# Two heads' softmax sums in one operation, and GpSimd's share of the weights given to ScalarE and VectorE

## The chip, the cores and the metric

The kernel runs on one core of one Trainium2 chip. Its time is device microseconds of one execution; the time of a kernel is the median of several. The core's engines work side by side, each through its own queue in order: TensorE (PE), VectorE (DVE), ScalarE (ACT), GpSimd (POOL) and SyncE (SP), which starts most of the DMAs. Some DMAs are started from ACT's queue.

## The reference

Attention over 4 batches of 8 heads, 576 positions of 64 values, with a learned relative bias; its output goes through a layer of three matrices with a maximum, and then a gated layer:

```python
scores = scale * np.matmul(q, k.transpose(0, 1, 3, 2))
...
scores = scores + bias.transpose(2, 0, 1)[None, :, :, :]
scores = scores - np.max(scores, axis=-1, keepdims=True)
attn = np.exp(scores)
attn = attn / (np.sum(attn, axis=-1, keepdims=True) + 1e-09)
return np.matmul(attn, v)
...
h = np.maximum(np.maximum(x @ w1, x @ w2), x @ w3) @ w_out
out = (sigmoid(h @ w_gate) * (h @ w_val)) @ moe2_w_out
```

All is float32; for the fast matrix products most operands are written as a sum of two 16-bit parts, a high and a low one.

## The kernel before, in words

The bias of all heads is made first and written to memory (to about 98 us). Then the attention runs in 160 steps. A *unit* is a tile of 128 (the last of a head 64) rows of one head; the units of two heads, an even and an odd one, alternate, so ten units make a *decade*: both heads of pair P, tiles 0 to 4, units 10P to 10P+9. Units u and u+1 with u even have the same rows of two heads. The 40 units of the first batch (`by_pe`, heads 0 to 7) go another way than the 120 after them.

The order on all queues is written out by hand: the loop `for u in range(NU + 7)` (L928) issues step u, and each helper takes the unit that is due in that step. In step u there are, in this order: `emit_E(u)` (DVE, L637: minimum of bias and scores, out of the accumulator memory), `emit_X(u)` (ACT, L643: the exponential, which also sums the row into `l`), the load of a later bias tile (ACT's queue), `emit_S(u+1)` (PE: scores, L617 and L618), `emit_r1(u-1)` (DVE, L648: the sum is scaled), `emit_hi2`, `emit_lo` and `emit_T` of units due, `emit_hi(u-1)` (DVE, L657: the reciprocal, and then the high part of the weights), evacuations of matrix products that are ready (`flush`), the product with v (`emit_V`), `prep(u)`, and then `feed.step`, which issues as much of the first layer of the batch before (`moe1`) as fills the step on PE. The fill is set by a table (`FEED`, 2.6 to 2.7 us a step) and doesn't look at what happens on the chip.

For the units after the first batch the weights go in one of two ways. Mostly ACT writes the high part out of exponential and reciprocal in step u+1 (L662), and DVE the low part in step u+2 (`emit_lo`, L677: product minus high part), and SP then starts a transposing DMA (`emit_T`, L702) from the weight buffer `ph` (five of them, `NPH`) to `pt`, from which PE takes its product with v. Where `by_pool(u)` is true (three of ten units in the second batch, two of ten in the third and fourth, 28 in all) GpSimd scales the exponential in place (L659), ACT casts it into the high part (L668), GpSimd subtracts (L674), and the transposing DMA is issued in step u+5. In the first batch GpSimd scales (L659 also) and PE transposes (`emit_TP`, L690).

`prep(u)` spreads the preparation of later heads over the steps. With s counted so that pair P's step s is u = 10P - 16 + s: SP loads q at s = 0 and k at s = 1 (`load_qk`, L359 and L360), into one buffer; ACT takes squares of them at s = 2 and 3 (`qk_squares`, L371); later DVE and POOL split them (L407, L402), SP transposes them (`r_trans`, L411) at the next decade's s = 0 and 1, and DVE swaps the halves of the transposed keys for each head (`k_swap`, L421 and L422) at s = 14 (even head) and 15 (odd head). The scores of the new pair's first two units need these: they are issued in the steps after. Because 10P - 16 is even, q is loaded in an even step and k in an odd one. For the pairs 2 to 5 the loads are issued six steps earlier; for pairs 6 to 15, ten decades, as said here.

What sets the lags: `e` tiles 4, `ph` tiles 5, two tiles of scores, and one tile each for raw q and k.

Of the kernel before, what the change touches and what calls it, by code (L numbers as in the profile page):

```python
# [10 lines left out]
F32 = mybir.dt.float32  # L11
# [3 lines left out]
AF = mybir.ActivationFunctionType  # L15
ALU = mybir.AluOpType
# [16 lines left out]
ESC = 16384.0  # L33
# [31 lines left out]
def tile_kernel(ctx, tc, q, k, v, w1, b1, w2, mw1, mw2, mw3, mwo, gw, vw, ow, xtab, masks, out):  # L65
    nc = tc.nc
# [38 lines left out]
    def tiny(n=1):  # L105
        for _ in range(min(n, len(tq))):
            tq.pop(0)()

    def end_tiny():
        tiny(len(tq))  # L110
# [26 lines left out]
    def take_sums():  # L137
        for then, g in summed:
            then(g)
        del summed[:]  # L140
# [20 lines left out]
    with tc.manual_schedule():  # L161
# [3 lines left out]
        PPB = H // 2  # L165
# [27 lines left out]
        def rpool(name, bufs):  # L193
            return at.enter_context(tc.tile_pool(name=name, bufs=bufs, side="right"))

        p1, p2, p3, p4 = rpool("p1", 1), rpool("p2", 2), rpool("p3", 3), rpool("p4", 4)
# [142 lines left out]
        def by_pe(n):  # L339
            return n < H  # L340
# [166 lines left out]
        units = []  # L507
# [3 lines left out]
        bias_t, e_t, ph_t, l_t, r_t, pt_t = {}, {}, {}, {}, {}, {}  # L511
# [93 lines left out]


        s_t, v_rest = {}, []

        def emit_S(u):

            n, it = units[u]
            m = rows[it]
            kq, k2 = kq_t[n], k2_t[n]
            ps = ps_s.tile([128, 1024], F32, tag="s", name="s")
            qs = kq[:, it, 0, :m]
            for j, kk in enumerate((kq[:, :, 1], k2)):
                nc.tensor.matmul(ps[:m, 0:512], lhsT=qs, rhs=kk[:, 0:4], start=(j == 0), stop=(j == 1))  # L617
                nc.tensor.matmul(ps[:m, 512:576], lhsT=qs, rhs=kk[:, 4, 0:64], start=(j == 0), stop=(j == 1))  # L618
            put_sums(ps[:, 600:616])
            s_t[u] = ps  # L620

        ep_t, x_t, n_ep = {}, {}, [0]

        def new_ep(u):
            ep_t[u] = ep_buf[n_ep[0] % len(ep_buf)]
            n_ep[0] += 1
            return ep_t[u]

        def emit_E(u):

            n, it = units[u]
            m = rows[it]
            ps = s_t.pop(u)
            e = new_ep(u)[:, 0:S] if by_pe(n) else p4.tile([128, S], F32, tag="e", name="e", bufs=NE)
            mx = p4.tile([128, 1], F32, tag="mx", name="mx")
            l = p4.tile([128, 1], F32, tag="l", name="l")
            nc.vector.tensor_tensor_reduce(e[:m], ps[:m, :S], bias_t.pop(u)[:m], -1.0, 3.0e38, ALU.add, ALU.min, mx[:m])  # L637
            e_t[u], l_t[u], x_t[u] = e, l, mx
            take_sums()

        def emit_X(u):
            m = rows[units[u][1]]
            nc.scalar.activation(e_t[u][:m], e_t[u][:m], AF.Exp, scale=-1.0, bias=x_t.pop(u)[:m], accum_out=l_t[u][:m])  # L643

        def emit_r1(u):
            m = rows[units[u][1]]
            r_t[u] = p4.tile([128, 1], F32, tag="r", name="r")
            nc.vector.tensor_scalar(r_t[u][:m], l_t.pop(u)[:m], 1e-9, 1.0 / ESC, op0=ALU.add, op1=ALU.mult)  # L648

        def by_pool(u):  # L650

            return u % 10 in ((2, 5, 8) if u < 20 * PPB else (2, 5)) and not by_pe(units[u][0])

        def emit_hi(u):
            m = rows[units[u][1]]
            r = r_t[u]
            nc.vector.reciprocal(r[:m], r[:m])  # L657
            if by_pool(u) or by_pe(units[u][0]):
                nc.gpsimd.tensor_scalar(e_t[u][:m], e_t[u][:m], r[:m], 1.0, op0=ALU.mult, op1=ALU.mult)  # L659
                return  # L660
            ph_t[u] = p3.tile([128, 2, S], F16, tag="ph", name="ph", bufs=NPH)
            nc.scalar.activation(ph_t[u][:m, 0], e_t[u][:m], AF.Copy, scale=r[:m])  # L662
# [7 lines left out]
        def emit_lo(u):  # L670
            m = rows[units[u][1]]
            ph = ph_t[u]
            if by_pool(u):
                nc.gpsimd.tensor_tensor(ph[:m, 1], e_t.pop(u)[:m], ph[:m, 0], op=ALU.subtract)  # L674
                r_t.pop(u)
            else:
                nc.vector.scalar_tensor_tensor(ph[:m, 1], e_t.pop(u)[:m], r_t.pop(u)[:m], ph[:m, 0], op0=ALU.mult, op1=ALU.subtract)  # L677
# [17 lines left out]
        def emit_T(u):  # L695
            n, it = units[u]
            m = rows[it]
            g, i0 = (0, 0) if it < 2 else (1, 2)
            if (n, g) not in pt_t:
                pt_t[n, g] = p1.tile([128, 9, (256, 320)[g]], F16, tag=f"pt{g}{n % 2}", name="pt")  # L700
            c0 = 128 * (it - i0)
            nc.sync.dma_start_transpose(out=pt_t[n, g][:, :, c0:c0 + m], in_=ph_t.pop(u)[:m].rearrange("p a s -> p (a s)"))  # L702
# [222 lines left out]
        def at_step(u, off):  # L925
            return [u - off] if 0 <= u - off < NU else []

        for u in range(NU + 7):  # L928
            t = FEED[u // (10 * PPB)]
            flush(both=False)  # L930
            if u == 10 * PPB + FIRST_MOE:
                flush()
                while late3:
                    late3.pop(0)[1]()
                psT.close()
                pools.update(mm=psA.enter_context(tc.tile_pool(name="ps_mm", bufs=4, space=PSUM)), n=4)
            if u == 0:
                emit_S(0)
            while late3 and late3[0][0] <= u:
                late3.pop(0)[1]()  # L940
            if u < NU:
                emit_E(u)
            for x in at_step(u, 0):
                emit_X(x)
            if u < NU:
                load_bias(u + NBI)
                t -= 0.49
            if u + 1 < NU:
                emit_S(u + 1)
            if v_rest:  # L950
                v_rest.pop(0)(u)
            tiny()
            for x in at_step(u, 1):
                emit_r1(x)
            for x in at_step(u, 5):
                if by_pool(x):
                    emit_T(x)
            for x in at_step(u, 2):
                emit_hi2(x)
                if not (by_pe(units[x][0]) or by_pool(x)):  # L960
                    emit_lo(x)
                    emit_T(x)
            tiny()
            for x in at_step(u, 1):
                emit_hi(x)
            for x in at_step(u, 3):
                if by_pool(x):
                    emit_lo(x)
                elif by_pe(units[x][0]):
                    emit_TP(x)  # L970
            flush()
            if slow:
                slow.pop(0)()
            for ua, g, late_, pe2 in ((3, 0, LA, False), (9, 1, LB, False), (3, 0, LA0, True), (9, 1, LB0, True)):
                w = u - ua - late_
                if w >= 0 and w % 10 == 0 and w // 10 < NP:
                    P = w // 10
                    if pe2 != (by_pe(2 * P) and by_pe(2 * P + 1)):
                        continue
                    if g == 0 and P % PPB == 0 and P // PPB >= 2:  # L980
                        while len(feed.q) > 1:
                            feed.one()
                        flush()
                        while slow:
                            slow.pop(0)()
                    emit_V(P, g, u)
                    if g == 1 and P % PPB == PPB - 1 and P < NP - 1:
                        xfer = P // PPB, max(u + (1 if P < PPB else 2), 10 * PPB + FIRST_MOE)
                    t -= (1.9, 2.3)[g]
            if xfer is not None and u >= xfer[1]:  # L990
                feed.q.append(moe1(xfer[0], x2[xfer[0]]))
                xfer = None
            prep(u)
            if u == 34:
                for _ in side_work:
                    force_ring()
                    end_tiny()
                common_scales()
            if u >= 6 and u % 2 == 0:
                next(side_work, None)  # L1000
            if u == 10 * PPB:
                w64_o = [t.bitcast(I32).rearrange("p (f t) -> p f t", t=2) for t in
                         (slots[3][:, 1536:3072], fx2[:, 0:1536], fx2[:, 1536:3072], fx2[:, 0:1536])]
                out_work = first_weights((3,), w64_o, {3: quarters(fx2[:, 3072:6144])}, 2)
                next(out_work)
            if u >= 10 * PPB + OUT_AT:
                next(out_work, None)
            feed.step(t)
# [265 lines left out]
```

## Time and profile before

| | us |
|---|---|
| three runs | 1093.58, 1082.88, 1083.96 |
| median | 1083.96 |
| profiled execution, its time | 1085.36 |
| its span, first to last instruction | 1083.5 |
| PE busy in the span | 995.3 |
| DVE busy | 689.5 |
| ACT busy | 549.1 |
| POOL busy | 189.1 |

An engine's busy time is a sum over stages; what counts in a stage is which wait ends last there. A row of a timeline gives start, duration, engine, line and operation, output and inputs, and in brackets the idle time before it with what ended it. PE, DVE, ACT, POOL stand for the engines, SPq for the queue of SP, whose rows are the starts of DMAs.

### The profile page before, as it was taken

How to read it: one execution, taken by the hardware profiler on the slowest of the kernel's cores; microseconds unless marked ns; L12 is line 12 of the kernel's file. 1: busy time of each engine (PE TensorE's matmuls, PEld its weight loads, DVE VectorE, ACT ScalarE, POOL GpSimd, SP SyncE). 2: the span in 40 equal slices, each digit the busy share in tenths (PEclk: the TensorE clock that was granted, in tenths of full speed). 3: DMA queues.
4: the chain of work that ended last, by engine and by line, in shares of the span. 5: the costliest groups of instructions: out<-in, count | busy, mean ns of one | idle time of the engine just before them, and what ended most of it. 6: DMA issues, size and time to landing. Idle time of an engine off the chain costs nothing.

```text
span 1083.5 us, 20167 instructions
## 1 busy us (share of the span) xinstructions
PE 995.3 (92%) x7620; PEld 659.7 (61%) x7620; DVE 689.5 (64%) x1764; ACT 549.1 (51%) x1089; POOL 189.1 (17%) x199
## 2 busy tenths in 40 slices
PE   6977889878898899889999999998999999999998
PEld 2223445556665567656777777776764666766743
DVE  7997768889986889878866867778521221322210
ACT  6997778666775767776654435534410111211100
POOL 1003544343432244223321100000000000000000
PEclk9998989989998999999999999999999999999999
DMA  7898878999999999989964332323001000000001
GB/s 226 298 262 236 192 194 224 248 230 183 222 249 198 185 222 242 243 176 213 212 135 128 108 96 79 111 85 97 1 10 38 12 10 11 10 11 10 11 20 39
DMA packets 242958, 148.53 MB, mean 137 GB/s; under 512 B 183085, under 2 KB 214061, under 8 KB 242861
## 3 DMA queue, kind: packets, MB, share of 16 engines
q1 hardware_dynamic: 221604, 104.77, 45.2%
q10 hardware_dynamic: 21256, 42.48, 14.6%
q8 instruction: 60, 0.98, 0.4%
q14 instruction: 38, 0.30, 0.1%
HBM read 89.53 MB, written 15.34 MB: 97 GB/s over the span
## 4 chain that ended last, share of the span: by engine, by line
PE 53%; DVE 21%; DMA 10%; ACT 7%; issue 5%; ACTq 1%; POOL 1%; SPq 1%; DVEq 0%; POOLq 0%
PE po L1212 13%; PE mm L797 12%; PE pg L797 8%; PE pvl L797 8%; DMA pt<-ph 5%; PE s L797 3%; PE s L617 3%; PE t L690 2%; PE mm L756 2%; PE mm L752 2%; DVE xT L543 2%; DMA bias<-bias_d 2%; DVE e L637 2%; ACT ph L662 1%; DVE gT L1187 1%
## 5 line engine op out<-in xcount | busy, mean ns | idle before, releaser
L797 PEld LDWEIGHTS <-slot 128*128 128x128 f16 x2304 | 221.4, 99 | 88.2 <-issue 25.3
L797 PE MATMUL mm<-xT,slot 128*128 128x288 f16 x1512 | 212.1, 294 | 14.4 <-ACT hm L818 10.4
L1212 PE MATMUL po<-OW,gT 128*128 128x512 f16 x648 | 141.3, 379 | 0.0
L797 PEld LDWEIGHTS <-GW 128*128 128x128 f16 x1152 | 112.8, 98 | 41.7 <-issue 8.9
L797 PEld LDWEIGHTS <-VW 128*128 128x128 f16 x1152 | 112.2, 98 | 28.3
L643 ACT ACTIVATE e<-e,mx 128x576 f32<-128x576 f32 (+1 forms) x120 | 92.5, 771 | 46.2 <-DVE mx L637 42.5
L797 PE MATMUL pg<-x,GW 128*128 128x288 f16 x864 | 113.4, 289 | 0.5 <-DVE x_e L154 0.5
L797 PE MATMUL pvl<-x,VW 128*128 128x288 f16 x864 | 111.7, 286 | 0.0
L1177 ACT ACTIVATE sg<-pg,ug 128x576 f32<-128x576 f32 x48 | 35.5, 739 | 145.0 <-PE pg L797 131.4
L1212 PEld LDWEIGHTS <-gT 128*128 128x128 f16 x648 | 63.4, 98 | 74.8
L1184 DVE SCALAR_TENSOR_TENSOR sg<-pvl,sg 128x576 f32<-128x576 f32 x48 | 36.2, 754 | 108.4 <-PE pvl L797 107.6
L677 DVE SCALAR_TENSOR_TENSOR ph<-e,r,ph 128x576 f16<-128x576 f32 (+1 forms) x92 | 83.1, 903 | 22.5 <-ACT ph L662 22.3
L637 DVE CUSTOM_DVE_ANT_0 e<-s,bias 128x576 f32<-128x576 f32 (+1 forms) x120 | 89.5, 746 | 7.9 <-DMA bias<-bias_d 5.1
L1186 ACT CAST gT<-sg 128x576 f16<-128x576 f32 x48 | 32.2, 672 | 107.1 <-DVE sg L1184 107.1
L662 ACT ACTIVATE ph<-e,r 128x576 f16<-128x576 f32 (+1 forms) x92 | 71.0, 772 | 22.0 <-DMA pt<-ph 11.2
L552 PE MATMUL bo<-xT,w2blk 128*32 128x512 f32 x192 | 60.3, 622 | 16.9 <-DVE xT L543 14.3
L617 PE MATMUL s<-k,kq 128*128 128x512 f16 (+1 forms) x160 | 63.1, 394 | 13.2 <-DVE k L422 13.2
L1217 DVE TENSOR_TENSOR ob<-po,uo 128x512 f32<-128x512 f32 x16 | 11.1, 692 | 96.8 <-PE po L1212 96.8
L617 PE MATMUL s<-kq 128*128 128x512 f16 (+1 forms) x160 | 63.9, 399 | 8.4 <-DVE mx L637 5.9
L797 PE MATMUL mm<-hT,slot 128*128 128x288 f16 x504 | 66.1, 286 | 0.0
L1187 DVE TENSOR_TENSOR gT<-sg,gT 128x576 f16<-128x576 f32 x48 | 36.4, 759 | 34.9 <-ACT gT L1186 34.9
L617 PEld LDWEIGHTS <-kq 128*128 128x128 f16 (+1 forms) x320 | 32.7, 102 | 39.5 <-issue 17.4
(203 smaller groups left out, 1652.0 us busy)
## 6 DMA issues: line engine op xcount, KB each, us to landing
bias<-bias_d ACTq DMA_DIRECT2D x128, 288.0 KB, 4.1
bias_d<-x SPq DMA_DIRECT2D x36, 288.0 KB, 4.3
x<-in_moe_w_dram SPq DMA_DIRECT2D x12, 768.0 KB, 6.5
w<-in_moe_w_gate_dram SPq DMA_DIRECT2D x12, 512.0 KB, 3.8
w<-in_moe_w_val_dram SPq DMA_DIRECT2D x12, 512.0 KB, 3.6
w<-in_moe_w_out_dram SPq DMA_DIRECT2D x12, 512.0 KB, 3.4
bias<-bias_d ACTq DMA_DIRECT2D x32, 144.0 KB, 4.7
out_dram<-ob SPq DMA_DIRECT2D x36, 128.0 KB, 2.3
```

The costliest lines, as they stand in the source:

```text
L552: nc.tensor.matmul(bo[32 * g:32 * g + 32, 0:512], lhsT=lhsT, rhs=hs[4 * ti + g][:, :, 0:128], start=True, stop=True, tile_position=(0, 32 ...
L617: nc.tensor.matmul(ps[:m, 0:512], lhsT=qs, rhs=kk[:, 0:4], start=(j == 0), stop=(j == 1))
L637: nc.vector.tensor_tensor_reduce(e[:m], ps[:m, :S], bias_t.pop(u)[:m], -1.0, 3.0e38, ALU.add, ALU.min, mx[:m])
L643: nc.scalar.activation(e_t[u][:m], e_t[u][:m], AF.Exp, scale=-1.0, bias=x_t.pop(u)[:m], accum_out=l_t[u][:m])
L662: nc.scalar.activation(ph_t[u][:m, 0], e_t[u][:m], AF.Copy, scale=r[:m])
L677: nc.vector.scalar_tensor_tensor(ph[:m, 1], e_t.pop(u)[:m], r_t.pop(u)[:m], ph[:m, 0], op0=ALU.mult, op1=ALU.subtract)
L797: nc.tensor.matmul(ps[hf][:, :HS], lhsT=W(wp, kk), rhs=X(xp, kk)[:, hf * HS:(hf + 1) * HS], start=(first and i == 0), stop=(last and i == 2))
L1177: nc.scalar.activation(hm3(sg), pg[:, :, :HS], AF.Sigmoid, scale=ugm)
L1184: nc.vector.scalar_tensor_tensor(hm3(sg), pvl[:, :, :HS], DOWN2, hm3(sg), op0=ALU.mult, op1=ALU.mult)
L1186: nc.scalar.copy(gT[:, 0, m, c0:c0 + S], sg)
L1187: nc.vector.tensor_tensor(gT[:, 1, m, c0:c0 + S], sg, gT[:, 0, m, c0:c0 + S], op=ALU.subtract)
L1212: nc.tensor.matmul(po[:, 0, :], lhsT=gT[:, gi, kk, 128 * ct:128 * ct + 128], rhs=OW[:, wi, kk], start=(i == 0), stop=(i == 3 * K2 - 1))
```

## The change

The sum column `l` and the reciprocal `r` become tiles of two columns, one for each head of a pair of units. The scaling of sums and the reciprocal are done once for both, in the even step after the odd unit. `emit_hi` is issued for both units there, the odd one first; in the odd step that follows, `emit_lo` and `emit_T` are issued for both, the even one first. In the first batch the even unit's GpSimd scaling so moves one step later and behind the odd one's; `emit_TP` stays where it is. `by_pool` is false for every unit, so that from the second batch on ACT writes all high parts and DVE all low parts.

```diff
@@ emit_E @@
-            l = p4.tile([128, 1], F32, tag="l", name="l")
+            if u % 2 == 0:
+                l = p4.tile([128, 2], F32, tag="l", name="l")
+                l_t[u], l_t[u + 1] = l[:, 0:1], l[:, 1:2]
+                l2_t[u] = l
@@ emit_r1 @@
-            r_t[u] = p4.tile([128, 1], F32, tag="r", name="r")
-            nc.vector.tensor_scalar(r_t[u][:m], l_t.pop(u)[:m], 1e-9, 1.0 / ESC, op0=ALU.add, op1=ALU.mult)
+            if u % 2 == 0:
+                return
+            r = p4.tile([128, 2], F32, tag="r", name="r")
+            nc.vector.tensor_scalar(r[:m], l2_t.pop(u - 1)[:m], 1e-9, 1.0 / ESC, op0=ALU.add, op1=ALU.mult)
+            r_t[u - 1], r_t[u] = r[:, 0:1], r[:, 1:2]
+            r2_t[u] = r
@@ by_pool @@
-            return u % 10 in ((2, 5, 8) if u < 20 * PPB else (2, 5)) and not by_pe(units[u][0])
+            return False
@@ emit_hi @@
-            nc.vector.reciprocal(r[:m], r[:m])
+            if u in r2_t:
+                r2 = r2_t.pop(u)
+                nc.vector.reciprocal(r2[:m], r2[:m])
@@ step u @@
             for x in at_step(u, 2):
                 emit_hi2(x)
-                if not (by_pe(units[x][0]) or by_pool(x)):
-                    emit_lo(x)
-                    emit_T(x)
+            if u % 2:
+                for x in at_step(u, 3) + at_step(u, 2):
+                    if not (by_pe(units[x][0]) or by_pool(x)):
+                        emit_lo(x)
+                        emit_T(x)
             tiny()
             for x in at_step(u, 1):
-                emit_hi(x)
+                if x % 2:
+                    emit_hi(x)
+                    emit_hi(x - 1)
```

## Rows read from the trace of the kernel before

**Rows 1.** Busy time by stage, batches two to four (columns in the first line).

```profile
core 0: us, PE busy (x) PEld busy (x) DVE busy (x) ACT busy (x) POOL busy (x), PEclk, DMA share, GB/s
...
182.10:311.70 129.60, 110.85 (x892) 75.03 (x893) 114.11 (x311) 87.73 (x190) 50.63 (x46) 0.93 1.12 222
311.70:438.00 126.30, 114.10 (x978) 80.35 (x976) 104.93 (x302) 88.22 (x189) 41.18 (x39) 0.96 1.13 216
438.00:557.00 119.00, 110.12 (x965) 78.30 (x963) 100.90 (x290) 82.68 (x174) 36.55 (x36) 0.99 1.06 205
```

**Rows 2.** Waits in total: us, times, longest us.

```profile
PE s L617 <- DVE k L422: 13.2, 10, 2.8
...
ACT ph L662 <- DMA pt<-ph: 11.2, 5, 5.2
...
ACT junk_w L371 <- DMA rqk<-in_k_dram: 7.9, 6, 2.3
```

**Rows 3.** Groups of instructions: count, busy us, mean ns, idle before.

```profile
L677 DVE SCALAR_TENSOR_TENSOR ph<-e,r,ph 128x576 f16<-128x576 f32 (+1 forms) x92 | 83.1, 903 | 22.5 <-ACT ph L662 22.3
L662 ACT ACTIVATE ph<-e,r 128x576 f16<-128x576 f32 (+1 forms) x92 | 71.0, 772 | 22.0 <-DMA pt<-ph 11.2 <-ACT e L643 3.9 <-DVE R L407 1.9
...
L756 PE MATMUL mm<-pt,vh 128*64 128x256 f16 (+1 forms) x672 | 48.0, 294 | 7.1 <-DMA pt<-ph 4.3 <-ACT xT L855 1.5 <-DVE r L657 1.1
...
L674 POOL TENSOR_TENSOR ph<-e,ph 128x576 f16<-128x576 f32 (+1 forms) x28 | 37.1, 1326 | 35.4 <-ACT ph L668 30.5 <-DMA bias<-bias_d 4.5
...
L657 DVE RECIPROCAL r<-r 128x1 f32<-128x1 f32 (+1 forms) x160 | 24.9, 156 | 1.8
```

**Rows 4.** Timelines of DVE and of POOL, around 306 us.

```profile
306.25 1.26 DVE L677 SCALAR_TENSOR_TENSOR ph<-e,r,ph 128x576 f16<-128x576 f32 x1 [1.08 <-ACT ph L662]
...
305.62 1.28 POOL L674 TENSOR_TENSOR ph<-e,ph 128x576 f16<-128x576 f32 x1
```

**Rows 5.** Timeline of SP's queue, steps 102 to 105.

```profile
386.54 5.65 SPq L702 DMA_TRANSPOSE pt<-ph  x3
392.28 0.54 SPq L359 DMA_DIRECT2D rqk<-in_q_dram  x1
...
393.59 1.93 SPq L411 DMA_TRANSPOSE kq<-R  x1
395.62 3.14 SPq L702 DMA_TRANSPOSE pt<-ph  x1
398.81 0.58 SPq L359 DMA_DIRECT2D rqk<-in_k_dram  x1
```

**Rows 6.** Timeline of ACT, steps 107 and 108.

```profile
404.57 0.74 ACT L371 ACTIVATE junk_w<-rqk 128x640 bf16<-128x640 f32 x1 [1.06 <-DMA rqk<-in_k_dram]
...
405.30 0.76 ACT L643 ACTIVATE e<-e,mx 64x576 f32<-64x576 f32 x1
...
406.06 0.76 ACT L662 ACTIVATE ph<-e,r 128x576 f16<-128x576 f32 x1
```

**Rows 7.** Timeline of DVE, steps 103 and 109.

```profile
387.76 0.74 DVE L637 CUSTOM_DVE_ANT_0 e<-s,bias 128x576 f32<-128x576 f32 x1
...
407.07 0.80 DVE L677 SCALAR_TENSOR_TENSOR ph<-e,r,ph 128x576 f16<-128x576 f32 x1
...
408.47 0.48 DVE L422 COPY k<-kq 64x640 f16<-64x640 f16 x1
```

**Rows 8.** Timeline of PE, scores of unit 111.

```profile
409.23 0.38 PE L617 MATMUL s<-k,kq 128*128 128x512 f16 x1
```

**Rows 9.** A long wait of PE, and the stage of 6 us behind it.

```profile
343.29 3.18 PE L797 MATMUL mm<-xT,slot 128*128 128x288 f16 x12 [4.27 <-ACT hm L818]
...
342.00:348.00 6.00, 4.71 (x21) 2.67 (x21) 3.08 (x15) 3.19 (x6) 0.80 (x1) 0.54 1.14 226
```

**Rows 10.** Timelines of PE and POOL in the first batch, units 0, 1, 26, 27.

```profile
102.90 0.76 PE L690 MATMUL t<-hT,x 128*128 128x128 f32 x5 [1.10 <-POOL x L659]
...
104.16 2.74 POOL L659 TENSOR_SCALAR x<-x,r 128x576 f32<-128x576 f32 x3
...
159.21 0.74 POOL L659 TENSOR_SCALAR x<-x,r 128x576 f32<-128x576 f32 x1 [1.13 <-DVE r L657]
...
162.04 0.74 PE L690 MATMUL t<-hT,x 128*128 128x128 f32 x5 [0.35 <-ACT xT L692]
```

More of the change, by code (lines that the diff above doesn't have):

```diff
@@ L607, in tile_kernel @@
         s_t, v_rest = {}, []
+        l2_t, r2_t = {}, {}
         def emit_S(u):
@@ L635, in emit_E @@
             mx = p4.tile([128, 1], F32, tag="mx", name="mx")
-            l = p4.tile([128, 1], F32, tag="l", name="l")
+            if u % 2 == 0:
+                l = p4.tile([128, 2], F32, tag="l", name="l")
+                l_t[u], l_t[u + 1] = l[:, 0:1], l[:, 1:2]
+                l2_t[u] = l
             nc.vector.tensor_tensor_reduce(e[:m], ps[:m, :S], bias_t.pop(u)[:m], -1.0, 3.0e38, ALU.add, ALU.min, mx[:m])
-            e_t[u], l_t[u], x_t[u] = e, l, mx
+            e_t[u], x_t[u] = e, mx
             take_sums()
@@ L642, in emit_X @@
             m = rows[units[u][1]]
-            nc.scalar.activation(e_t[u][:m], e_t[u][:m], AF.Exp, scale=-1.0, bias=x_t.pop(u)[:m], accum_out=l_t[u][:m])
+            nc.scalar.activation(e_t[u][:m], e_t[u][:m], AF.Exp, scale=-1.0, bias=x_t.pop(u)[:m], accum_out=l_t.pop(u)[:m])
         def emit_r1(u):
             m = rows[units[u][1]]
-            r_t[u] = p4.tile([128, 1], F32, tag="r", name="r")
-            nc.vector.tensor_scalar(r_t[u][:m], l_t.pop(u)[:m], 1e-9, 1.0 / ESC, op0=ALU.add, op1=ALU.mult)
+            if u % 2 == 0:
[4 more added lines that the diff above has]
+            r2_t[u] = r
         def by_pool(u):
-            return u % 10 in ((2, 5, 8) if u < 20 * PPB else (2, 5)) and not by_pe(units[u][0])
+            return False
         def emit_hi(u):
```

## Prediction, made blind

> **What bounds the kernel now.** I read the page's slices and its busy table first, then the busy time by stage, then the waits in total, then the groups of instructions, and last the timelines of all queues over one stretch of ten steps. The busy time by stage [rows 1] shows the three batches that the change touches (heads 8 to 31, 40 steps each, a step being one tile of one head): they last 129.6, 126.3 and 119.0 us, 3.1 us a step. TensorE is busy for 111, 114 and 110 us of them and VectorE for 114, 105 and 101 us, so both are near the bound and ScalarE (88, 88, 83 us) is not. After 557 us TensorE works almost alone and nothing is changed there; time comes or goes only where TensorE is made to wait in these batches. The waits in total [rows 2] say for what it waits: 13.2 us in ten waits of the scores for the second VectorE copy of the swapped keys (L422). ScalarE waits 7.9 us in six for loaded keys (the squares, L371), and 11.2 us in five for a weight buffer that a transposing DMA still reads. That chain of loads and transposes goes over SP's queue, and the timeline of SP [rows 5] shows what a sum of compute engines does not: from 386.54 to beyond 398.81 us SP starts one transfer as soon as the last is handed over. Three transposes take it 5.65 us (1.88 each), another one 3.14.
>
> **The change, part by part.** The sum is made against the profiled execution, 1085.36 us (span 1083.5, and 1.9 around it); that is 1.4 above the median of 1083.96, so I take 1.4 off at the end.
>
> *Work moved off GpSimd.* 28 units (12, 8 and 8 in the three batches) lose a GpSimd scaling, a ScalarE cast and a GpSimd subtraction, and get a scaled copy on ScalarE (0.772 us) and a subtraction on VectorE [rows 3]. ScalarE: one pass replaces another; the difference is between 0 and 28 x 0.77 = 21.6 us. I take near 0, as both write the same 576 columns, and ScalarE's 36 to 42 us of idle time a batch [rows 1] cover it. VectorE: a subtraction alone takes 0.80 us [rows 7], so 28 x 0.80 = 22.4 us are added. Against it stands that the mean of the 92 present ones is 903 ns [rows 3]: 92 x 0.103 = 9.5 us are lost to something. The pair of rows in [rows 4] shows to what: one that began at 306.25, while GpSimd subtracted until 306.90, took 1.26 us, 0.65 of it beside GpSimd. Other GpSimd work stays, so the relief is between 0 and 9.5 us; I take 7.
>
> The Trainium skill, page "SBUF — State Buffer", section "SBUF: two separate sides", says that the port pair which VectorE and GpSimd share is an exclusive lock for a whole instruction. The rows agree for this pair; by the rule alone the relief would be 28 x 0.46 = 13 us, 6 us more than taken, and the sum would not move, since VectorE's net load is hidden in it anyway.
>
> *Small operations.* 60 pairs of steps lose one reciprocal and one scaling of sums each. A reciprocal is 156 ns in the group [rows 3], and a scaling is taken alike. Alone that is up to 120 x 0.156 = 18.7 us; but now they stood behind a subtraction and overlapped with it, while in the new order they follow one another, so it may also be 0. I take 4. An operation of two columns is priced as one of one. VectorE's net: 22.4 - 7 - 4 = +11 us over 120 steps, 0.1 us a step. Its idle time (16, 21 and 18 us a batch, rows 1) covers that; were the cover gone, it would be +11, and at the worst ends +22.
>
> *GpSimd's detour.* A GpSimd unit hands its transposing DMA to SP two steps after the others, and holds its weight buffer longer. That explains part of the 11.2 us of ScalarE waits, and 4.3 us in which the attention product waited for a transposed tile [rows 2, 3]. Between 0 and 4.3 + 4.27 us (the second is the wait in [rows 9]) of TensorE's idle time can go; buffers are also held longer by the pairing, so I take 5. As the second of these waits ended, the granted clock fell to 0.54 in the next 6 us, near the lower of the two levels (1.2 of 2.4 GHz): 6 us x 0.46 = 2.8 us lost again, which would also go, twice 2.8 if both waits do.
>
> *Pairing, batch 0.* The even head's scaling is now issued one step later and behind the odd head's. At the start [rows 10] TensorE already waits 1.10 us for the first scaling and starts at 102.90. The second starts at 104.16; without the first in front (0.74) it starts at 103.4, ends 0.91 later and the first ends at 105.2: +2.4 us. Later there is room: unit 27 ended at 159.95, unit 26 behind it would end at 160.7, and its transposes run at 162.04. Between 0 and 3; I take +2.5.
>
> *Pairing, later batches.* Here lies the loss. In the even step ScalarE now does exp(u), then the weights of u-1, then of u-2; in the odd step VectorE subtracts twice and then swaps keys; SP gets both transposes in the odd step. Once in ten steps, in an odd one, the key load is issued on SP behind that step's transposes: behind one before, behind two now. ScalarE's squares of those keys are queued before the next exp, and so before both weight copies of that pair. VectorE's two subtractions wait for these, and the key swap of the second head is queued behind them; TensorE's scores of the next pair wait for the swap. I replay steps 103 to 111 with the old durations. Step 103 starts at 387.76 [rows 7]; the minimum pass (0.68) and one subtraction (0.80) bring the first transpose to 389.24. Two take 3.76 and end at 393.0; the query load with what is behind it takes 1.31 (392.28 to 393.59), the key transpose 2.03 (393.59 to 395.62) [rows 5], then two transposes again: 400.1. The key load was issued at 398.81, so it is 1.3 later. From issue to the squares it was 5.76 (404.57, rows 6): squares at 405.9. Squares to exp 0.73, exp 0.76 [rows 6], two copies 0.68 and 0.77, two subtractions of 0.73 each, two swap copies of 0.5: 411.4 with the gaps between engines. It was 408.95 [rows 7], and the scores of unit 111 started at 409.23 [rows 8], 0.28 later. So unit 111 is 2.2 us late. If SP's transposes cost nothing more, 0.6; if the latter two take 3.14 each, 4.7. A saving is excluded where squares wait now.
>
> How often? ScalarE waited six times for keys [rows 2], so I count six decades of the ten: 13.2 us. The other four get between 0 and 2.2 each from the same queue; I take 0.8, together 3.2. In these four the swap of the first head comes earlier, since no subtraction stands ahead of it in its even step; their share of the 13.2 us is 5.3, gained (in the six it is already inside the replay). The new waits are 1.5 + 2.2 = 3.7 us long. In [rows 9] a wait of 4.27 was followed by the lower clock; for a shorter wait I take 1 us each, 6 in all, against 5.6 given back above.
>
> Sum: 13.2 + 3.2 - 5.3 - 5 + 2.5 + 6 - 5.6 = +9, and 2 for the part of VectorE's 11 us that falls into steps where it is late already: +11. 1085.4 + 11 - 1.4 = **1095 us**, slower by about 1%.
>
> The Trainium skill, page "DMA: Bandwidth & Descriptors", section "Issuing engines are not separate DMA queues", calls the sequencer's time to start a DMA usually small beside the DMA. Here it is not: 1.88 us for a start [rows 5]. By that rule the 1.3 us of the replay fall away, which is rival B.
>
> **The rivals.** A: faster. TensorE waits for the swap now because the first head's swap stands behind a subtraction that waits for ScalarE; the change takes it from there, and ends the detour. If the load of keys comes in time, all of the 13.2, the 4.3 and the 4.27 us go and batch 0 costs 2.5: 1084 - 19 = 1065. For it: the two longest kinds of wait are both touched. Against: SP has no spare time just ahead of the load. It decides if the keys land within 1.3 us of now. B: no change. SP's queue is shorter than its rows say, because starting overlaps with the transfers before it: the six decades lose 0.9 instead of 2.2, 7.8 less in all: 1087. Against: SP's rows stand end to end. C: clearly slower. All ten decades lose 2.2 (22 us), the buffers bring nothing and VectorE becomes the bound in the first of these batches (114 of 129.6 us busy): 22 + 2.5 = 1084 + 25 = 1109. For it: VectorE gets 12 x 0.80 us there. Against: its idle time covers that on the mean. D: the change doesn't relieve VectorE, since its slow subtractions stand beside other GpSimd work: then 7 us come back, mostly hidden; it lies within the range of the forecast.
>
> **How the numbers follow.** Forecast 0.45, A 0.27, B 0.12, C and what goes with it 0.16. A measurement tells about 1% (10.8 us) from no change. The forecast case reaches from 1086 to 1106 (per decade 0.6 to 4.7) and gives 0.28 to slower and 0.17 to the same; B goes to the same, C to slower: faster 0.27, same 0.29, slower 0.44. Half of A and a little of C's upper side are left out: 1066 to 1110.
>
> **What would show it.** Right: about ten waits of TensorE on L422 of 3 to 4 us, on the odd head, where ten of 1.3 stand now; ScalarE's wait for loaded keys well above 7.9 us; VectorE's subtraction at some 0.83 us in the mean, 120 of them; SP's two transposes back to back ahead of the key load. Wrong: if the waits on L422 shrink and the three batches get shorter, the load came in time (A). If VectorE is busy for over 120 us of the first of these batches and waits for nothing, C. If batch 0 is as long as before, its 2.5 us were absorbed.

## The result and the profile after

The changed kernel takes 1095.95 us in the median against 1084.51 us of the kernel before, in six runs each. The ratio on record is 1.0119, 95% interval [1.0083, 1.0154]: it is slower by 1.2%, and 1095 us was forecast. (The ratios here and below are those on record; they leave out single executions of 1969 to 5048 us, which occurred with three of the kernels, and differ by up to 0.2% from the quotient of two medians, here 1.0105.) The profiled execution took 1096.02 us, with a span of 1094.2.

Busy time by stage, kernel after: batch one, then batches two to four (columns as in [rows 1]; the batches end at other times than before, so each stage is cut at its own step).

```profile
99.20:177.80 78.60, 68.19 (x475) 37.75 (x472) 59.11 (x180) 64.67 (x146) 43.85 (x59) 0.96 0.85 214
177.80:315.00 137.20, 110.93 (x895) 74.59 (x894) 116.72 (x282) 88.25 (x190) 24.13 (x24) 0.96 1.04 217
315.00:444.80 129.80, 114.50 (x976) 80.50 (x976) 110.53 (x270) 87.77 (x190) 23.86 (x22) 0.96 1.05 214
444.80:567.00 122.20, 111.50 (x958) 78.78 (x958) 106.00 (x257) 79.44 (x170) 20.96 (x20) 0.97 1.01 193
```

The loss lies in batches two to four: 137.2, 129.8 and 122.2 us where 129.6, 126.3 and 119.0 stood [rows 1]. From one step to the same step (40 to 159) it is 388.4 against 374.1 us, 14.3 more in this pair of executions. TensorE and ScalarE are busy for about as long as before; VectorE is busy for 2.6 to 5.6 us more a batch and still idle for 16 to 21. So nothing became the bound; something is waited for.

The waits in total, kernel after (us, times, longest us):

```profile
DVE ph L687 <- ACT ph L672: 37.0, 32, 3.3
...
ACT junk_w L371 <- DMA rqk<-in_k_dram: 34.1, 10, 4.4
...
PE s L618 <- DVE k L422: 13.9, 12, 2.0
PE s L618 <- DVE mx L641: 13.7, 9, 3.1
...
PE mm L807 <- ACT hm L828: 12.4, 5, 4.7
PE mm L807 <- DVE xT L773: 7.1, 7, 2.2
```

The second row answers to the last of [rows 2]: ScalarE waits for loaded keys 34.1 us in ten, where it was 7.9 in six. Against that, its squares of the queries, at the same line, waited in the kernel before:

```profile
ACT junk_w L371 <- DMA rqk<-in_q_dram: 16.0, 8, 3.0
```

After, that is 0.4 us. For both loads together ScalarE so waits 34.5 us where it was 23.9: not only longer, but at another place, ahead of the keys' squares, with the weight copies behind them. VectorE's subtractions then wait for the weight copies 37.0 us (22.3 in [rows 3]). At the end stands TensorE, but not where I had expected it: its waits for the swapped keys (L422) are 13.9 us against 13.2. What grew are small waits behind the same two queues: for the minimum (mx) 13.7 us against 5.9, for the evacuations hm and xT 12.4 and 7.1 against 10.4 and 3.1, and for the sums of squares (L130) 3.0 against 0.9. The waits put down to weight buffers and transposed tiles (`pt<-ph` in [rows 2, 3]) are gone; what the former were is said below, under GpSimd's detour.

### The profile page after: what moved, and what is told of

Same layout as the page of the kernel before. It is cut to its first block, busy times and chain, and to the rows that moved or that the text cites. A ratio compares the mean times of both kernels' runs of the same rounds, so it can differ in the third digit from the quotient of the medians.

```text
span 1094.2 us, 19838 instructions
## 1 busy us (share of the span) xinstructions
PE 997.0 (91%) x7620; PEld 660.7 (60%) x7620; DVE 698.6 (64%) x1632; ACT 547.5 (50%) x1089; POOL 129.2 (12%) x143
## 3 DMA queue, kind: packets, MB, share of 16 engines
q10 hardware_dynamic: 21256, 42.48, 13.9%
## 4 chain that ended last, share of the span: by engine, by line
PE 38%; DVE 10%; ACT 3%; issue 1%; ACTq 0%; DVEq 0%
PE po L1226 13%; PE pg L807 8%; PE pvl L807 8%; PE mm L807 5%; PE s L807 3%; DVE gT L1201 1%; DVE wf L93 1%; DVE sg L1198 1%; ACT gT L1200 1%; DVE wf L95 1%; DVE wf L91 1%; DVE ph L687 1%; ACT sg L1191 1%; PE mm L766 1%; DVE wf L1106 1%
## 5 line engine op out<-in xcount | busy, mean ns | idle before, releaser
L807 PE MATMUL mm<-xT,slot 128*128 128x288 f16 x1512 | 214.0, 296 | 20.2 <-ACT hm L828 12.4
L647 ACT ACTIVATE e<-e,mx 128x576 f32<-128x576 f32 (+1 forms) x120 | 92.8, 773 | 65.8 <-DVE mx L641 34.1
L687 DVE SCALAR_TENSOR_TENSOR ph<-e,r,ph 128x576 f16<-128x576 f32 (+1 forms) x120 | 100.9, 882 | 37.3 <-ACT ph L672 37.0
L672 ACT ACTIVATE ph<-e,r 128x576 f16<-128x576 f32 (+1 forms) x120 | 86.0, 764 | 13.6 <-DVE hm L830 6.1
L618 PE MATMUL s<-kq 128*128 128x512 f16 (+1 forms) x160 | 63.6, 398 | 16.3 <-DVE mx L641 13.7
L552 PE MATMUL bo<-xT,w2blk 128*32 128x512 f32 x192 | 62.3, 633 | 16.8 <-DVE xT L543 13.2
L618 PE MATMUL s<-k,kq 128*128 128x512 f16 (+1 forms) x160 | 62.7, 392 | 14.0 <-DVE k L422 13.9
L836 POOL TENSOR_TENSOR hT<-hm,hT 128x576 f16<-128x576 f32 x24 | 36.1, 1506 | 220.8 <-ACT hT L835 185.8
```

Source lines behind the costliest of these rows:

```text
L552: nc.tensor.matmul(bo[32 * g:32 * g + 32, 0:512], lhsT=lhsT, rhs=hs[4 * ti + g][:, :, 0:128], start=True, stop=True, tile_position=(0, 32 ...
L807: nc.tensor.matmul(ps[hf][:, :HS], lhsT=W(wp, kk), rhs=X(xp, kk)[:, hf * HS:(hf + 1) * HS], start=(first and i == 0), stop=(last and i == 2))
```

## The experiments

Ratios are against the kernel before, on the same chip; line numbers are those of each kernel and differ by a few. The theories that the expectations speak of: the changed kernel loses time because (1) the key load stands later in SP's queue; (2) of the order of work on ScalarE and VectorE that pairing makes, two copies and two subtractions at a time with the key swap behind them; (3) VectorE has 28 subtractions more; and, formed from e10, (4) GpSimd's third unit of each decade had kept a transposing DMA from ahead of the key load.

| kernel | median us | ratio and interval | ScalarE's wait for keys, us |
|---|---|---|---|
| before (first six runs) | 1084.51 | 1 | 7.9 |
| after | 1095.95 | 1.0119 [1.0083, 1.0154] | 34.1 |
| e1 after, keys first | 1086.25 | 1.0028 [0.9991, 1.0065] | 9.9 |
| e2 before, GpSimd off | 1088.85 | 1.0043 [1.0005, 1.0080] | 17.4 |
| e3 after, swap first | 1091.34 | 1.0051 [1.0011, 1.0091] | 26.6 |
| e4 after, squares late | 1093.37 | 1.0084 [1.0048, 1.0119] | at other operations |
| e5 after, keys and swap first | 1086.46 | 1.0022 [0.9990, 1.0054] | 9.0 |
| e6 before, GpSimd off, keys first | 1082.38 | 0.9993 [0.9960, 1.0025] | 2.7 |
| e7 before, keys first | 1087.47 | 1.0049 [1.0014, 1.0083] | at other operations |
| e8 as e6, swap first too | 1085.33 | 1.0033 [0.9997, 1.0069] | 3.4 |
| e9 before, keys later | 1100.34 | 1.0156 [1.0104, 1.0208] | 35.9 |
| e10 pairing alone | 1082.13 | 0.9989 [0.9951, 1.0028] | 16.3 |
| e11 after, GpSimd for third units | 1079.14 | 0.9973 [0.9945, 1.0000] | 18.4 |
| e12 after, GpSimd for the others | 1098.61 | 1.0150 [1.0110, 1.0190] | 30.8 |

**e1: the key load ahead of the transposing DMAs of its step** (pairs 6 to 15; it moves ahead of two entries of SP's queue, and nothing else changes).

```diff
+            Pk, sk = divmod(u + QLEAD, 10)
+            if sk == 1 and 6 <= Pk < NP:
+                load_qk(Pk, 1)
             if u % 2:
                 for x in at_step(u, 3) + at_step(u, 2):
@@ prep @@
-                    load_qk(Pq, s)
+                    if s == 0 or Pq < 6:
+                        load_qk(Pq, s)
```

> The changed kernel, with the load of k for pairs 6 to 15 issued on SP ahead of the two transposes of its step. Theory 1 (late keys: ScalarE's wait for the key load holds up both weight copies and the evacuations behind them): the wait for loaded keys falls from 34.1 us to under 12, and the time from 1096 to 1082 to 1088. Theory 2 (the pairs themselves: two copies and two subtractions in one step delay what is queued behind them, keys or not): the wait falls, but the time stays at 1092 to 1097. Theory 3 (VectorE's 28 more subtractions are the cost): as theory 2.

The ratio falls from 1.0119 to 1.0028, with intervals that don't touch: some three quarters of the loss go by the place of one load. Timelines of SP's queue in the same decade (start us, us), first kernel after, then e1:

```profile
394.43 0.70 SPq L359 DMA_DIRECT2D rqk<-in_q_dram  x1
...
395.89 1.75 SPq L411 DMA_TRANSPOSE kq<-R  x1
397.73 4.80 SPq L712 DMA_TRANSPOSE pt<-ph  x2
402.59 0.57 SPq L359 DMA_DIRECT2D rqk<-in_k_dram  x1
```

```profile
393.20 0.54 SPq L359 DMA_DIRECT2D rqk<-in_q_dram  x1
...
394.50 1.72 SPq L411 DMA_TRANSPOSE kq<-R  x1
396.27 0.83 SPq L359 DMA_DIRECT2D rqk<-in_k_dram  x1
```

From query load to key load it is 8.16 us after, 6.53 before [rows 5], and 3.07 in e1. The 1.63 us between before and after come with the second transposing DMA: two starts take SP 4.80 us, where one took 3.14.

**e2: GpSimd off alone** (the kernel before, no pairing).

```diff
-            return u % 10 in ((2, 5, 8) if u < 20 * PPB else (2, 5)) and not by_pe(units[u][0])
+            return False
```

> The kernel before, with by_pool false for all units and nothing paired. Theories 1 and 2 (the pairing costs): as fast as before or faster, 1074 to 1085, ScalarE's 11 us of waits for weight buffers gone, its wait for keys near 8 us. Theory 3 (the added subtractions cost): 1092 or more.

0.4% slower, with an interval that begins just above 1, so this half of the change is no gain; the time lies between the two expectations and meets neither. TensorE's wait for a transposed tile went, as in the whole change, and the subtractions have a mean of 820 ns (903 in [rows 3]), but ScalarE now waits for keys 17.4 us. Its weight copies still wait, for longer than the 11.2 us of [rows 2]; they are only put down to another DMA, whose data they don't read:

```profile
ACT ph L662 <- DMA rqk<-in_q_dram: 22.6, 6, 5.6
```

**e3: the odd head's key swap ahead of the two subtractions.**

```diff
+            Pk, sk = divmod(u + 1, 10)
+            if sk == 0 and 5 <= Pk < NP:
+                k_swap(2 * Pk + 1)
             if u % 2:
                 for x in at_step(u, 3) + at_step(u, 2):
@@ prep @@
-                if s in (sw, sw + 1):
+                if s == sw or s == sw + 1 and Pq < 5:
```

> The changed kernel, with the key swap of the odd head (from pair 5 on) issued on VectorE ahead of the two subtractions of its step. As the prediction had it (the loss goes through the swap): TensorE's 13.9 us of waits on L422 fall by 8 or more, time 1084 to 1089. Theory 1 in its other form (the loss goes through the evacuation on ScalarE and the sums of squares): L422 falls, other waits of TensorE grow, time within 4 us of 1096.

It takes back some 0.7 of the 1.2% (the intervals of the two kernels overlap a little, at 1.0083 to 1.0091), and lies between the two expectations. The keys are still late (26.6 us); the waits on L422 fall to 8.1 us.

**e4: the squares of the keys one step later**, so that ScalarE doesn't stand still for them.

```diff
-                elif s in (2, 3):
+                elif s == 2 or s == 3 and Pq < 6:
                     qk_squares(Pq, s - 2)
                 elif s == 4:
+                    if Pq >= 6:
+                        qk_squares(Pq, 1)
                     qk_scales(Pq)
```

> The changed kernel, with ScalarE's squares of the keys (pairs 6 to 15) issued one step later, behind the two weight copies. Theory 1: VectorE's wait for weights falls from 37 us to under 28; TensorE still waits for the sums of these squares; 3 to 9 us faster than 1096. Theory 2: within 3 us of 1096.

ScalarE's wait goes, and TensorE's sums of squares (L130) wait for ScalarE 9.1 us instead of 3.0. At 1.0084 it can't be told from the change. It is a miss for the thought that ScalarE's standing still was by itself the cost: the late keys then stop TensorE by the next link.

**e5: e1 and e3 together.**

> The changed kernel with both: the keys' load ahead of the transposes and the odd head's swap ahead of the subtractions. If lateness of keys and of the swap are two parts of one path, both together bring little over the first alone: 1080 to 1087. If they are two paths, the sum of both gains: 1074 to 1080.

1.0022 against e1's 1.0028: the swap adds nothing that can be told once the keys are early. So both edits cut one path, at two places.

**e6, e7 and e8: the same edits without the pairing.** e6 is e2 with the key load first, e8 the same with the swap first, e7 the kernel before with the key load first and GpSimd on.

> The kernel before with by_pool false, nothing paired, and the keys' load ahead of the one transpose of its step. Theory 1 (late keys also explain why GpSimd off alone gained nothing, its wait for keys being 17.4 us against 7.9): wait for keys under 8 us, time 1076 to 1084, faster than before. Theory 3 (VectorE's added subtractions cost by themselves): 1086 or more, whatever the keys do.

> The kernel before with only the keys' load ahead of its step's transpose. Theory 1: the wait for keys was hardly on the path there (7.9 us in six waits), so 0 to 5 us faster, 1080 to 1085. If the keys were on the path in the kernel before as well: 1074 to 1079.

> As the unpaired run with the keys first, and the odd head's swap ahead of the subtraction of its step. Theory 1: TensorE's waits on L422 under 8 us, 1074 to 1082. If the swap matters only behind two subtractions: within 3 us of the unpaired run with the keys first.

e6 is level with the kernel before, although VectorE has all 28 subtractions more and GpSimd none of these units: that leaves theory 3 little to explain, unless the earlier keys gain just what the subtractions cost, which e11 and e12 decide. e8 is no faster than e6: unpaired, the swap's place gains nothing. e7 is a miss. I thought that keys loaded earlier could only help, and it is 0.5% slower. Its waits show where it may have gone (us, times, longest us):

```profile
ACT ph L663 <- DMA pt<-ph: 20.2, 8, 5.5
ACT junk_w L371 <- DMA kq<-R: 18.7, 6, 6.3
...
PE s L618 <- DVE k L422: 15.4, 6, 5.0
PE mm L798 <- DVE xT L764: 13.2, 10, 3.4
```

ScalarE's weight copies wait 20.2 us for transposing DMAs where it was 11.2 [rows 2], and TensorE waits 13.2 us for the evacuation xT where it was 3.1. The second row is hardly new: it stands in the main at the squares of the queries, which had waited 16.0 us before, put down to their load. An earlier place for one entry of SP's queue is a later one for those behind it. That this is what costs the 0.5% was not tried by itself.

**e9: the keys later in the kernel before**, by one step and two transposing DMAs (the second head's keys, and one weight tile more), with nothing of the change.

```diff
-                if s in (0, 1) and not 2 <= Pq <= 5:
+                if s == 0 and not 2 <= Pq <= 5 or s == 1 and Pq < 2:
                     load_qk(Pq, s)
-                elif s in (2, 3):
+                if s == 2 and Pq >= 6:
+                    load_qk(Pq, 1)
+                if s in (2, 3):
```

> The kernel before, with nothing of the change; only the load of the keys of pairs 6 to 15 is issued one step later, in an even step, behind that step's transposing DMA. Theory 1 (what the change costs is that loaded keys come later behind SP's transposes): ScalarE's wait for loaded keys goes from 7.9 us to over 25 us in ten, and the kernel becomes 0.6 to 1.2% slower, as the changed kernel is, with no operation added to VectorE and none paired. Theory 2 (the cost is the pairing itself, in the order of ScalarE's and VectorE's work): the kernel is within 0.3% of the kernel before, since a wait of 3 us once in ten steps is taken up by work that is queued ahead.

1.6% slower, and ScalarE waits for the keys 35.9 us in ten: late keys make the whole of such a loss with nothing paired and nothing moved between engines.

**e10: pairing alone** (the changed kernel with `by_pool` as before).

> The changed kernel with the GpSimd units left as they were before (28 units of the last three batches scaled and subtracted by GpSimd): pairing alone. If the two parts add up, it is 1.2 less 0.4, so 0.5 to 1.0% slower than the kernel before, with 92 subtractions on VectorE at a mean near 900 ns. Theory 1 expects ScalarE's wait for loaded keys above 15 us in it, since two of SP's transposes stand ahead of the key load in most decades. The rival (the parts hurt only together, through VectorE's 28 added subtractions) expects it within 0.3% of the kernel before.

No loss, 0.9989: neither the loss that adding up the parts gave nor the second transposing DMA of theory 1 came. The parts don't add up: -0.1 and +0.4 make +1.2%. The timeline of SP's queue in e10, in the same decade, shows why:

```profile
386.56 0.74 SPq L359 DMA_DIRECT2D rqk<-in_q_dram  x1
...
388.06 1.64 SPq L411 DMA_TRANSPOSE kq<-R  x1
389.79 2.74 SPq L712 DMA_TRANSPOSE pt<-ph  x1
392.59 0.58 SPq L359 DMA_DIRECT2D rqk<-in_k_dram  x1
```

One transposing DMA of weights stands between query and key load, not two, and so in all ten decades. The key load is issued in the sixth step of a decade, where the transposes of the third and fourth unit are due as a pair. The third unit (u % 10 = 2) is a GpSimd unit in all three batches, and hands over its DMA two steps later. Pairing alone so leaves one; GpSimd off alone puts the third unit's ahead of the query load; both together put two between query and key load. That is theory 4, and two kernels tell it from theory 3.

**e11 and e12: GpSimd kept for the third unit alone, and for the others alone** (both with the pairing).

```diff
-            return False
+            return u % 10 == 2 and not by_pe(units[u][0])
@@ e12 @@
-            return False
+            return u % 10 in ((5, 8) if u < 20 * PPB else (5,)) and not by_pe(units[u][0])
```

> The changed kernel with GpSimd kept for one unit in ten alone, the third of each decade (u % 10 == 2, 12 units of the last three batches). That unit's transposing DMA then goes to SP two steps later, and only one stands between the query load and the key load instead of two. Theory 4 (GpSimd's third unit kept a transposing DMA from ahead of the key load; taking it away is what turned the pairing into a loss): within 0.4% of the kernel before, ScalarE's wait for loaded keys under 20 us, though 16 of the 28 units are now VectorE's. Rival (the loss is VectorE's added work, in proportion to it): 16 of 28 units, so 0.6 to 0.8% slower.

> The counterpart: the changed kernel with GpSimd kept for the other 16 units (u % 10 of 5, and of 8 too in the first of these batches), and the third unit of each decade left to ScalarE and VectorE as in the change. Two transposing DMAs stand between query load and key load. Theory 4: still 0.8 to 1.3% slower than the kernel before, ScalarE's wait for loaded keys over 28 us, though only 12 units were added to VectorE. Rival (VectorE's added work): 12 of 28 units, so 0.3 to 0.6% slower.

Timelines of SP's queue, e11 and then e12; behind them a row of the waits in total of each, in the same order.

```profile
383.96 0.75 SPq L359 DMA_DIRECT2D rqk<-in_q_dram  x1
...
387.13 3.38 SPq L712 DMA_TRANSPOSE pt<-ph  x1
390.57 0.58 SPq L359 DMA_DIRECT2D rqk<-in_k_dram  x1
```

```profile
399.89 1.03 SPq L359 DMA_DIRECT2D rqk<-in_q_dram  x1
...
403.91 3.37 SPq L712 DMA_TRANSPOSE pt<-ph  x2
407.33 0.85 SPq L359 DMA_DIRECT2D rqk<-in_k_dram  x1
```

```profile
ACT junk_w L371 <- DMA rqk<-in_k_dram: 18.4, 10, 3.7
```

```profile
ACT junk_w L371 <- DMA rqk<-in_k_dram: 30.8, 10, 4.8
```

With the third unit on GpSimd, 16 subtractions more on VectorE cost nothing: 0.9973, and the interval reaches just to 1. With the others on GpSimd, 12 more cost 1.5%. The intervals are far apart and in the order that theory 4 gave; VectorE's added work has the opposite order. Over the ten decades the query load stands ahead of the key load by 6.8 us in the mean before, 7.6 after and in e12 7.5, 6.0 in e11, 3.4 in e1, and 10.5 in e9. The loss is not in proportion to that distance, since the query load moves too. Counted from the start of the sixth step of the decade (its minimum pass), the key load starts in the mean after 6.2 us before, 5.9 in e10, 6.4 in e11 and 3.9 in e1, and these lose nothing that can be told. It starts after 7.1 us in e2, 7.6 in e3 and e12, 7.9 in the changed kernel, 8.2 in e4 and 9.4 in e9, and these lose 0.4 to 1.6%. e7, at 3.1, doesn't fit. The table's last column says much the same: up to some 18 us of ScalarE's waits for keys are free or nearly so (e10, e11; e2, at 17.4, costs 0.4%), and those of 31 to 36 us cost 1.2 to 1.6%.

## Why the prediction was right, and where it was not

The time, the sign and the start of the chain were right: SP's queue, two transposing DMAs ahead of the key load, ScalarE held at the squares with the weight copies behind. e1 and e9 show it from both sides. That the time came within 1 us is luck in part, as the steps show one by one:

**The replay.** It put the second swap's end at 411.4. Step 103 began at 389.20 instead of 387.76 [rows 7], 1.44 later, so it should be 412.84. Timelines of ScalarE, then VectorE, then TensorE, kernel after:

```profile
407.37 0.74 ACT L371 ACTIVATE junk_w<-rqk 128x640 bf16<-128x640 f32 x1 [3.91 <-DMA rqk<-in_k_dram]
...
408.87 1.43 ACT L672 ACTIVATE ph<-e,r 128x576 f16<-128x576 f32 x2
410.20 0.87 ACT L828 ACTIVATE hm<-mm,fac 128x288 f32<-128x288 f32 x2
```

```profile
410.33 1.55 DVE L687 SCALAR_TENSOR_TENSOR ph<-e,r,ph 128x576 f16<-128x576 f32 x2 [2.61 <-ACT ph L672]
...
412.40 0.48 DVE L422 COPY k<-kq 64x640 f16<-64x640 f16 x1
```

```profile
408.25 0.16 PE L130 MATMUL s<-ssq,ones 128*128 128x1 bf16 x1 [0.86 <-ACT junk_w L371]
...
410.73 3.19 PE L807 MATMUL mm<-xT,slot 128*128 128x288 f16 x12 [1.56 <-ACT hm L828]
...
414.00 0.38 PE L618 MATMUL s<-k,kq 128*128 128x512 f16 x1
```

The swap ended at 412.88, as replayed, but by two errors that cancel: the two starts took SP 4.80 us instead of 3.76, and the squares began 4.78 us after the key load instead of 5.76. What failed is the last step, "TensorE's scores of the next pair wait for the swap". TensorE lost its time earlier in the step: 0.86 us at the sums of squares and 1.56 at an evacuation that ScalarE does behind exp and two copies. The scores started at 414.00 without a wait. So ten waits of 3 to 4 us on L422 didn't come; there are twelve, of 2.0 at most. Each helper behind a held engine passes on part of the delay. That the swap's place is still on the path, e3 shows. Two slips in the working changed little: with the 0.28 us from swap to scores unit 111 is 2.45 us late and not 2.2, and at 4.7 us a decade the forecast case reaches to 1110 and not to 1106.

**Six decades.** The count was taken from where a wait stood before; it is ten. The four at 0.8 and the 5.3 us gained there by earlier first swaps were wrong too: L422 gave nothing back. In the sum, 13.2 + 3.2 - 5.3 makes 11, near the 11.4 us between the medians; but the rest of the sum came to nothing only because the detour's -5 stood against batch one's 2.5 and the 2 for VectorE, and no run shows any of the three as priced.

**GpSimd's detour, -5.** Its waits went, but the term has the wrong sign: alone it costs 0.4% (e2). I priced what the detour delayed, and not that the delay kept a transposing DMA out of the stretch that matters, although the order of the steps told which unit's it was (and in the kernel before the detour is three steps, u+5 against u+2, not two). And I put all of the loss on the pairing, which alone costs nothing (e10). Nor were the 11.2 us of [rows 2] in the main waits for a weight buffer: four of the five, 8.5 us, end with the start of a bias load, which stands ahead of the copy in ScalarE's queue and has no part in that buffer. The longest one, in the timeline of ScalarE's queue, kernel before (the operation ahead of these rows ends at 227.87):

```profile
232.51 0.45 ACTq L519 DMA_DIRECT2D bias<-bias_d  x1
233.08 0.77 ACT L662 ACTIVATE ph<-e,r 128x576 f16<-128x576 f32 x1 [5.21 <-DMA pt<-ph]
```

Why a bias load is held until another DMA lands the rows don't show. It was so as well for 15.4 of the 16.0 us ahead of the queries' squares before, and for five of the six waits of e2's weight copies. All ten waits for keys in the changed kernel end with the squares themselves, so the reading of these stands.

**VectorE.** The two rows that answer to those in [rows 3], kernel after:

```profile
L687 DVE SCALAR_TENSOR_TENSOR ph<-e,r,ph 128x576 f16<-128x576 f32 (+1 forms) x120 | 100.9, 882 | 37.3 <-ACT ph L672 37.0
...
L672 ACT ACTIVATE ph<-e,r 128x576 f16<-128x576 f32 (+1 forms) x120 | 86.0, 764 | 13.6 <-DVE hm L830 6.1 <-DMA rqk<-in_q_dram 4.5 <-DVE mx L641 2.0
```

The subtractions went from 83.1 to 100.9 us, 17.8 more (15.4 were forecast), and VectorE in all from 689.5 to 698.6, 9.1 more (forecast 11), hidden as said. The mean came to 882 ns rather than 830: the relief was small.

**Batch one, +2.5.** 78.6 us against 84.3 in the kernel before, 83.0 in e1 and, unpaired, 80.6 in e2: executions differ by more than the term, and no loss is seen. Over all traces the batch takes 78.2 to 84.6 us in the eight paired kernels and 80.0 to 84.3 in the six unpaired. The term was absorbed, or is too small.

**Clock.** The 6 us lost and the 5.6 given back were to cancel, and so they did: 0.93, 0.96 and 0.99 in [rows 1] became 0.96, 0.96 and 0.97.

**The rivals.** A asked for the keys within 1.3 us of now, and they were later: in the decade shown their load starts 13.39 us after step 103, where it was 11.05. e11 shows what A was worth where they aren't: 0.3%, not 1.8. B has SP's starts overlap with the transfers before them; but e11 and e12, which differ in one start ahead of the key load and in which units GpSimd has, stand 1.8% apart. The Trainium skill ("DMA: Bandwidth & Descriptors", section "Issuing engines are not separate DMA queues") calls a start usually small beside its DMA; the trace does not agree, with 4.80 us of SP's queue for two. C needed VectorE busy for over 120 us of batch two; it is 116.7, and idle for 20.

**What stays open.** How TensorE's loss divides among its small waits; why e7 is slower; why bias loads are held; whether the 0.3% that e1 leaves is a loss at all, as its interval reaches below 1; and whether e11 is faster than the kernel before, as its interval ends at 1.

## What to carry to other kernels

Before moving work between engines, write down the order in which one queue starts its DMAs, step by step, and see which entry comes to stand ahead of a load that a whole engine waits for. A slow detour may be what keeps that queue free; then two edits that each cost little alone can cost more than their sum, and here keeping the detour for one unit in ten was enough. Follow a late input through every operation queued behind it, since the engine at the end may lose its time at another link than the last.

## What was not expected of the hardware

VectorE can be held up beside GpSimd for far longer than one operation of GpSimd. In e10 a subtraction that takes 0.80 us alone took 3.65 while GpSimd ran three operations one after the other beside it and began a fourth (timelines of VectorE and of GpSimd, start us, us):

```profile
213.59 3.65 DVE L687 SCALAR_TENSOR_TENSOR ph<-e,r,ph 64x576 f16<-64x576 f32 x1
```

```profile
213.36 0.79 POOL L402 TENSOR_SCALAR R<-rqk,sqk 128x640 f16<-128x640 f32 x1
214.12 1.27 POOL L836 TENSOR_TENSOR hT<-hm,hT 128x576 f16<-128x576 f32 x1
215.36 1.26 POOL L684 TENSOR_TENSOR ph<-e,ph 64x576 f16<-64x576 f32 x1
216.61 2.18 POOL L402 TENSOR_SCALAR R<-rqk,sqk 128x640 f16<-128x640 f32 x1
```

The fourth, of the same kind as the first (0.79 us), took 2.18 itself.

The mean of the 92 subtractions is 1017 ns in e10, where GpSimd works beside pairs of them, and 820 in e2, where it does none of its own; the kernel is no slower for it. The rule of the Trainium skill that the prediction weighed ("SBUF — State Buffer", section "SBUF: two separate sides", a lock on the shared port pair) agrees in kind. That VectorE can be held over several of GpSimd's operations in a row is what these rows add; that it was the lock which held it is not shown by itself.
